# Low words behind the next scaling, the last pair's split inside the first FFN unit, and weight quarters loaded in two parts

## The chip, the cores and the metric

The kernel runs on one core of a Trainium2 chip. The metric is the device time of one execution in microseconds. Before the change the median of three runs is 844.63 us (843.42 to 845.4). Engines are called as in the profile: PE (TensorE matmul), PEld (its weight loads), DVE (VectorE), ACT (ScalarE), POOL (GpSimd), SP (SyncE, which here only issues DMAs).

## The reference

Three stages in a row, all in float32:

```
ret  = (q @ k.T / 8 * Dmat) @ v            # 4 batches x 8 heads, 576 tokens, head size 64; Dmat = gamma**(i-j) for i >= j
x    = ret as 2304 tokens x 512
h    = x @ w_in                            # FFN 1: 512 -> 2048
g    = (a0 + a1 h + a2 h^2 + a3 h^3) / (1 + |b0||h| + |b1| h^2 + 1e-6)
x2   = g @ w_out                           # 2048 -> 512
h2   = x2 @ w_in2;  y = (s * relu(h2)^2 + b) @ w_out2     # FFN 2
```

## The kernel before, in words

A full-precision product is built from three matmuls of a faster float type: each operand is cut into a high word and a low word, and the kernel multiplies high by low, low by high and high by high (`three`, L494 to L497). So every x, every g and every weight is written twice: an ACT copy rounds to the high word, and a subtraction (mostly on POOL) gives the low word.

**Retention** (`retention`, L214) works on 16 pairs p of two heads: batch p // 4, head pair p % 4. A pair's data come in two loads on the SP queue: `xT` (k and q, 576 KB, L256) and `vk` (v and k by chunks, 480 KB, L260), each in a ring of four buffers. The order is written out by hand with `pin` (keep in program order) on every engine. Iteration p of the loop at L407 holds, in this order:

- SP: the loads of pair p + 3, then a quarter of a raw weight tile (`next_quarter`, L143; 256 KB; 12 quarters in all, for weight tiles 0 to 2). The load of `xT` has to wait until `value_state(p - 1)` has read the buffer, the load of `vk` until `value_chunk(p - 1)` has.
- POOL: `scale(p + 2)` (L286), which multiplies v of pair p + 2 by decay factors and so waits for that pair's `vk` load.
- PE: `value_state(p)` (L350), `state(p + 1)` (L338, which reads the scaled v of pair p + 1), then `value_chunk(p)` (L358), and at the end `scores(p + 2)` (L315).
- ACT, DVE, POOL: one step (from p = 4 on) of `w_cut_in_halves` (L188), a generator of five steps per weight tile: bit arithmetic on DVE (L195, L199, L202), and twice per tile a high word on ACT (L165) with its low word on POOL (L166).
- DVE: the result x of pair p (L361); ACT: its high word `xh` (L365); POOL: its low word `xl` (L366). These two are `parts`, called straight after `value_chunk(p)`.

POOL therefore meets, in iteration p: `scale(p + 2)`, in some iterations a weight's low word, then `xl` of the same pair p. After the loop the steps of the weight cut that are still left are run off.

**FFN 1** (`ffn`, L443) goes through units u of 512 tokens and one 128-column tile of w_in. `emit_in` makes h on PE in one of four PSUM banks; `rational` (L540) is a chain over ACT (L546, L547, L549, L556, L558), POOL (L548) and DVE (L550, L551, L559 to L561), whose last step frees the bank; then g's words (L566, L568) and the products with w_out. The first three units are pinned as well. Unit 0 uses tokens 0 to 511, that is pairs 0 to 3 alone. On ACT and POOL it stands behind everything that retention issued, the last pair's `xh` and `xl` among it. **FFN 2** follows and is not touched.

Of the kernel before, what the change touches and what calls it, by code (L numbers as in the profile page):

```python
# [9 lines left out]
F32 = mybir.dt.float32  # L10
# [5 lines left out]
ALU = mybir.AluOpType  # L16
# [28 lines left out]
def retention_ffn_kernel(ctx, tc, a, b, s2, b2, w, qkv, maskv, gdec, out):  # L45
    nc = tc.nc
    B, H, S, D = SHAPE
    NT, DM = out.shape
    P = 128
# [7 lines left out]
    const = ctx.enter_context(tc.tile_pool(name="const", bufs=1))  # L57
# [11 lines left out]
    zeros = const.tile([P, P], F32, name="zeros")  # L69
    lnb = const.tile([P, 1], F32, name="lnb")  # L70
    expb = const.tile([P, 1], F32, name="expb")

    xh = xpool.tile([P, NC, NT], F32R, name="xh")
    xl = xpool.tile([P, NC, NT], F32R, name="xl")
# [4 lines left out]
    def f32(t):  # L79
        return t.bitcast(F32)  # L80
# [16 lines left out]
    def next_load(eng=nc.sync, pin=free):  # L97
        if w_ahead:
            loads[:] = loads[-1:] + [w_load(w_ahead.pop(0), eng, pin)]
# [27 lines left out]
    def w_place_raw(kf):  # L127
        w_raw[kf] = stg.tile([P, 2 * DM], I64, tag=raw_tag(kf), name=f"raw{kf}")
        return w_raw[kf]
# [8 lines left out]
    def next_quarter(pin):  # L138
        if quarters:
            kf, x = quarters.pop(0)  # L140
            t = w_raw[kf] if x else w_place_raw(kf)
            cols = slice(DM // 2 * x, DM // 2 * (x + 1))
            pin(nc.sync.dma_start(out=t[:, cols], in_=w[kf][:, cols]))  # L143

    def w_words(kf):
        words = w_raw[kf].bitcast(I32).rearrange("p (n two) -> p n two", two=2)
# [65 lines left out]
    NPAIR = len(pairs)  # L212

    def retention(actx):  # L214

        sbt = actx.enter_context(tc.tile_pool(name="sbt", bufs=2))
# [30 lines left out]
        pin = tc.keep_in_program_order  # L247
        pe = dve = pin
        rows = [slice(Q * j, Q * j + Q) for j in range(2)]
# [12 lines left out]
        def main_v(p):  # L262
            return vk[p][:, 0:NM].rearrange("p (c h d) -> p c h d", c=NMAIN, h=2)

        def tail_v(p):
            return vk[p][:, NM:MIX]
# [4 lines left out]
        def loads(p):  # L271
            if p < NPAIR:
                load_x(p)
                load_vk(p)
# [4 lines left out]
        def decay(hp):  # L279
            for k, (t0, t1) in enumerate(((P, 2 * P), (2 * P, 4 * P), (4 * P, S))):  # L280
                pin(nc.scalar.activation(odec[:, hp, t0:t1], odec[:, hp, 0:t1 - t0], AF.Copy, scale=powers[:, k, hp:hp + 1]))

        def scale(p, eng=nc.gpsimd):
            if p < NPAIR:
                hp = pairs[p][1]
                pin(eng.tensor_tensor(out=main_v(p), in0=main_v(p), op=ALU.mult,  # L286
                                      in1=vdec[:, :, 2 * hp:2 * hp + 2].unsqueeze(3).to_broadcast([P, NMAIN, 2, D])))

        def scale_tail(p):
            hp = pairs[p][1]  # L290
            pin(nc.scalar.activation(tail_v(p), tail_v(p), AF.Copy, scale=vdec_tail[:, hp:hp + 1]))
# [15 lines left out]
        def place(c):  # L307
            return 0 if c is None else Q + c * P
# [36 lines left out]
        def value_state(p):  # L345
            for c in range(1, NMAIN):

                cs = slice(c * P, S if c == NMAIN - 1 else (c + 1) * P)
                for r in rows:
                    pe(nc.tensor.matmul(pv[p][r, O0 + cs.start:O0 + cs.stop], lhsT=spre[p % 2][r, c - 1, :], rhs=xT[p][r, 1, cs],  # L350
                                        start=c in (1, NMAIN - 1), stop=True, skip_group_check=True))

        def value_chunk(p):
            bb, hp = pairs[p]
            v = main_v(p)
            for c, q0, q1 in [(c, c * P, S if c == NMAIN - 1 else (c + 1) * P) for c in range(NMAIN)] + [(None, NM, S)]:
                for j, r in enumerate(rows):
                    pe(nc.tensor.matmul(pv[p][r, O0 + q0:O0 + q1], lhsT=tail_v(p) if c is None else v[:, c, j, :],  # L358
                                        rhs=pm[p][:, j, place(c):place(c) + q1 - q0], start=False, stop=True, skip_group_check=True))
            x = sbt.tile([P, S], F32, tag="x", name=f"x{p}")  # L360
            dve(nc.vector.tensor_tensor(out=x, in0=pv[p][:, O0:O0 + S], in1=odec[:, hp], op=ALU.mult))  # L361
            xs = slice(bb * S, (bb + 1) * S)

            def parts():
                pin(nc.scalar.copy(xh[:, hp, xs], x))  # L365
                pin(nc.gpsimd.tensor_tensor(out=xl[:, hp, xs], in0=x, in1=f32(xh[:, hp, xs]), op=ALU.subtract))  # L366

            return parts

# [23 lines left out]
        steps = (s for kf in range(W_FIRST) for s in w_cut_in_halves(kf))  # L393
# [10 lines left out]
        tails()  # L404
        decay(0)
        scale(1)
        for p in range(NPAIR):  # L407
            if p:
                loads(p - 1 + IN_BUFS)
            for _ in range((1, 1, 2, 0)[p] if p < 4 else 1):  # L410
                next_quarter(pin)
            if p in (13, 14):
                next_load(nc.sync, pin)
            if p == 12:
                small_loads()
            scale(p + 2)
            value_state(p)
            if p == 0:
                scores(1)()

            if p < 2:
                parts = value_chunk(p)
            if p < NPAIR - 1:
                state(p + 1)
                scale_tail(p + 1)
            for _ in range((p > 3) + (p == 14)):
                next(steps, None)
            if p > 1:
                parts = value_chunk(p)
            parts()  # L430
            if p + 1 < NP:
                decay(p + 1)
            if p == 14:
                pin(nc.scalar.activation(babs, b_sb, AF.Abs))
                pin(nc.vector.tensor_scalar(aneg, a_sb, -1.0, None, op0=ALU.mult))
            if p + 2 < NPAIR:
                scores(p + 2)()
        for _ in steps:
            pass
        assert not quarters  # L440


    def ffn(fctx):  # L443
        accp = fctx.enter_context(tc.tile_pool(name="accp", bufs=1))
        gp = fctx.enter_context(tc.tile_pool(name="gp", bufs=1))

# [93 lines left out]
        def rational(u):  # L540

            pin = pe if u < 3 else free
            h = hps[u]
            ta, tq, tt = [tmp_tile(u, x) for x in ("ta", "tq", "tt")]
            with behind(*parts_at[1:2]):
                pin(nc.scalar.activation(ta, h, AF.Abs))  # L546
            pin(nc.scalar.activation(tq, ta, AF.Identity, bias=babs[:, 0:1], scale=babs[:, 1:2]))  # L547
            pin(nc.gpsimd.tensor_tensor(out=tq, in0=tq, in1=ta, op=ALU.mult))  # L548
            pin(nc.scalar.activation(tt, h, AF.Identity, bias=aneg[:, 2:3], scale=aneg[:, 3:4]))  # L549
            pin(nc.vector.tensor_tensor(out=tt, in0=tt, in1=h, op=ALU.mult))  # L550
            x = pin(nc.vector.scalar_tensor_tensor(out=tt, in0=tt, scalar=aneg[:, 1:2], in1=h, op0=ALU.add, op1=ALU.mult))  # L551
            if u == 2:
                third.append(x)
            if parts_of:
                parts_of.pop()(pe)
            pin(nc.scalar.activation(ta, tq, AF.Ln, bias=lnb, scale=QS))  # L556
            r = hps.pop(u)
            exp = pin(nc.scalar.activation(r, ta, AF.Exp, bias=expb, scale=-1.0))  # L558
            pin(nc.vector.scalar_tensor_tensor(out=tt, in0=tt, scalar=aneg[:, 0:1], in1=r, op0=ALU.add, op1=ALU.mult))  # L559
            pin(nc.vector.scalar_tensor_tensor(out=r, in0=tq, scalar=QC, in1=r, op0=ALU.add, op1=ALU.mult))  # L560
            end = pin(nc.vector.scalar_tensor_tensor(out=tt, in0=r, scalar=-2.0, in1=tt, op0=ALU.add, op1=ALU.mult))  # L561
            ends[:] = [end, exp, *ends[2:]]

            def parts(pin=free):
                gh, gl = g_tiles(u)
                parts_at.append(nc.scalar.copy(gh, tt))  # L566
                ends[1:] = [pin(parts_at[-1]),
                            pin(nc.gpsimd.tensor_tensor(out=gl, in0=tt, in1=f32(gh), op=ALU.subtract))]  # L568

            if u < 3:  # L570
                parts_of.append(parts)
            else:
                parts()
            if u == 3:
                with behind(*ends):
                    w_split_half(W_FIRST - 1, 1, free)
                del w_raw[W_FIRST - 1]
                next_load()
# [432 lines left out]
        for u in range(NU):  # L1011
# [14 lines left out]
            if final[0:1024].all() and len(sums) > (1 if u == NU - 1 else 2):  # L1026
                x = sums.pop(0)
# [25 lines left out]
    nc.vector.memset(lnb, QC * QS)  # L1053
    nc.vector.memset(expb, float(-24.0 * np.log(2.0)))
    with ExitStack() as actx:
        retention(actx)
    with ExitStack() as fctx:
        ffn(fctx)


_INS = ["moe_a", "moe_b", "moe2_s", "moe2_b"]
# [72 lines left out]
```

## Time and profile before

| | before |
|---|---|
| median of three runs | 844.63 us |
| the profiled execution: its time, its span | 845.24 us, 843.3 us |
| PE busy | 833.5 us (99%) |
| PEld, DVE, ACT, POOL busy | 703.6, 616.2, 600.1, 393.6 us |
| granted TensorE clock | 1.00 over the span |
| loaded and stored by DMA | 109.17 MB, mean 129 GB/s |

Times inside the profile count from the start of the span. A busy share says when an engine had an instruction in flight; matmuls overlap, so the pitch from one start to the next says more of PE than its busy time. "A <- B" in a list of waits reads "A stood idle until B was done"; "issue" is idle time that the profile can't lay to anything. SPq is the DMA queue of SyncE: a row of it is one issue, and "to landing" is the time from the issue until the data are there.

### The profile page before, as it was taken

Reading aid. Unit: us, or ns where it says so; the run is one execution under the profiler, and the core shown is the slowest. Engines: PE = TensorE matmul, PEld = TensorE weight load, DVE = VectorE, ACT = ScalarE, POOL = GpSimd, SP = SyncE. Lnnn points to the kernel's source line nnn. Section 1 sums busy time; section 2 is a strip of 40 time slices with the busy share of each in tenths; the row PEclk is TensorE's granted clock in tenths of the full one; section 3 lists DMA queues with packets and bytes.
Section 4 is the critical chain, followed back from the end, with each engine's and each line's share of the span. In section 5 each row is a group of like instructions: output and inputs, shape, how many; then the busy total and the mean of one; then the engine's idle time right before and its main releaser. Section 6 shows DMA issues by size and latency. Waiting matters only on the chain.

```text
span 843.3 us, 13082 instructions
## 1 busy us (share of the span) xinstructions
PE 833.5 (99%) x4966; PEld 703.6 (83%) x4966; DVE 616.2 (73%) x859; ACT 600.1 (71%) x991; POOL 393.6 (47%) x324
## 2 busy tenths in 40 slices
PE   8999999999999999999999999999999999999998
PEld 7887788888888888888888888888888888888887
DVE  4786987697798879789968867788777543444445
ACT  4446998687788778789979886686667766555553
POOL 3785675555567655548856423344235221111100
PEclk9999999999999999999999999999999999999999
DMA  9982120101102101101111377545699984444302
GB/s 343 346 318 88 50 101 1 64 37 50 51 1 101 49 2 51 50 1 51 51 51 33 68 249 250 191 168 167 224 310 365 232 241 150 149 150 150 126 0 100
DMA packets 38174, 109.17 MB, mean 129 GB/s; under 512 B 3936, under 2 KB 4704, under 8 KB 33504
## 3 DMA queue, kind: packets, MB, share of 16 engines
q1 hardware_dynamic: 27104, 79.44, 26.9%
q0 software_dynamic: 10864, 28.31, 11.8%
q8 instruction: 39, 0.64, 0.3%
q10 hardware_dynamic: 144, 0.59, 0.2%
q14 instruction: 23, 0.19, 0.1%
HBM read 75.30 MB, written 28.84 MB: 123 GB/s over the span
## 4 chain that ended last, share of the span: by engine, by line
PE 90%; DVE 4%; DMA 2%; POOL 1%; issue 1%; ACT 1%; SPq 0%; ACTq 0%; DVEq 0%; POOLq 0%
PE p L497 23%; PE o L497 23%; PE h L497 21%; PE hB L497 7%; PE hA L497 5%; PE hG L497 5%; PE ht L497 3%; PE hs L497 3%; DMA vk<-in_qkv_dram 2%; PE pv L358 1%; POOL vk L286 1%; DVE pm L328 1%; DVE tt L559 0%; PE sc L315 0%; PE pv L338 0%
## 5 line engine op out<-in xcount | busy, mean ns | idle before, releaser
L497 PE MATMUL h<-xh,w 128*128 128x512 f32 (+1 forms) x640 | 184.5, 368 | 0.0
L497 PE MATMUL o<-gh,w 128*128 128x512 f32 (+1 forms) x584 | 165.9, 369 | 0.0
L548 POOL TENSOR_TENSOR tq<-tq,ta 128x512 f32<-128x512 f32 x72 | 98.1, 1363 | 99.1 <-ACT tq L547 92.9
L815 DVE TENSOR_TENSOR acc<-acc,p 128x512 f32<-128x512 f32 (+1 forms) x127 | 86.3, 680 | 72.8 <-PE p L497 71.8
L497 PEld LDWEIGHTS h<-xh,w 128*128 128x128 f32 x640 | 116.2, 188 | 20.4
L497 PE MATMUL p<-w,gh 128*128 128x512 f32 (+1 forms) x338 | 124.3, 388 | 0.0
L497 PEld LDWEIGHTS o<-gh,w 128*128 128x128 f32 x584 | 106.1, 189 | 18.4
L497 PE MATMUL h<-xl,w 128*128 128x512 f32 (+1 forms) x320 | 118.2, 369 | 0.5 <-DVE tt L561 0.4
L497 PE MATMUL o<-gl,w 128*128 128x512 f32 (+1 forms) x292 | 107.8, 369 | 0.0
L568 POOL TENSOR_TENSOR gl<-tt,gh 128x512 fp32r<-128x512 f32 x66 | 92.8, 1407 | 30.4 <-ACT gh L566 25.9
L497 PE MATMUL p<-w,gx 128*128 128x512 f32 (+1 forms) x363 | 99.3, 387 | 0.0
L166 POOL TENSOR_TENSOR w<-raw,w 128x512 fp32r<-128x512 f32 x38 | 55.2, 1477 | 82.4 <-ACT w L165 29.0
L497 PEld LDWEIGHTS p<-w,gx 128*128 128x128 f32 x363 | 67.9, 188 | 13.9
L559 DVE SCALAR_TENSOR_TENSOR tt<-tt,aneg,h 128x512 f32<-128x512 f32 x72 | 53.5, 743 | 31.2 <-ACT h L558 30.9
L497 PEld LDWEIGHTS p<-w,gh 128*128 128x128 f32 x338 | 63.5, 188 | 13.1
L497 PEld LDWEIGHTS h<-xl,w 128*128 128x128 f32 x320 | 60.3, 188 | 11.8 <-DVE tt L561 1.1
L556 ACT ACTIVATE ta<-tq,lnb 128x512 f32<-128x512 f32 x72 | 52.3, 727 | 21.8 <-POOL tq L548 20.9
L497 PE MATMUL p<-w,gl 128*128 128x512 f32 (+1 forms) x169 | 65.5, 388 | 0.0
L779 ACT ACTIVATE ta<-hG 128x512 f32<-128x512 f32 x14 | 8.4, 598 | 76.9 <-PE hG L497 76.9
L497 PEld LDWEIGHTS o<-gl,w 128*128 128x128 f32 x292 | 55.1, 189 | 9.6 <-POOL gl L568 0.4
L550 DVE TENSOR_TENSOR tt<-tt,h 128x512 f32<-128x512 f32 x72 | 49.0, 681 | 18.3 <-ACT tt L549 18.0
L546 ACT ACTIVATE ta<-h 128x512 f32<-128x512 f32 x72 | 43.0, 597 | 24.3 <-PE h L497 23.9
(149 smaller groups left out, 1812.1 us busy)
## 6 DMA issues: line engine op xcount, KB each, us to landing
raw<-in_w_dram SPq DMA_DIRECT2D x29, 1024.0 KB, 5.3
ws<-w SPq DMA_DIRECT2D x32, 512.0 KB, 8.4
w<-ws POOLq DMA_DIRECT2D x32, 512.0 KB, 5.5
xT<-in_qkv_dram SPq DMA_DIRECT2D x15, 576.0 KB, 7.5
vk<-in_qkv_dram SPq DMA_DIRECT2D x16, 480.0 KB, 7.0
sf<-ss POOLq DMA_DIRECT2D x7, 1024.0 KB, 5.1
out_dram<-acc SPq DMA_DIRECT2D x17, 256.0 KB, 2.6
acc<-acc POOLq DMA_DIRECT2D x8, 512.0 KB, 4.6
```

The source lines that it names most:

```text
L166: pin(nc.gpsimd.tensor_tensor(out=dst[:, 1], in0=src, in1=f32(dst[:, 0]), op=ALU.subtract))
L286: pin(eng.tensor_tensor(out=main_v(p), in0=main_v(p), op=ALU.mult, in1=vdec[:, :, 2 * hp:2 * hp + 2].unsqueeze(3).to_broadcast([P, NMAIN, ...
L328: dve(nc.vector.tensor_tensor(out=t[:, :, 0:S], in0=sc[:, :, M0:M0 + S], op=ALU.mult, in1=mask.unsqueeze(1).to_broadcast([P, 2, S])))
L358: pe(nc.tensor.matmul(pv[p][r, O0 + q0:O0 + q1], lhsT=tail_v(p) if c is None else v[:, c, j, :], rhs=pm[p][:, j, place(c):place(c) + q1 - ...
L497: yield nc.tensor.matmul(ps, lhsT=lh, rhs=rh, start=start and x == 0, stop=stop and x == 2, skip_group_check=True)
L546: pin(nc.scalar.activation(ta, h, AF.Abs))
L548: pin(nc.gpsimd.tensor_tensor(out=tq, in0=tq, in1=ta, op=ALU.mult))
L550: pin(nc.vector.tensor_tensor(out=tt, in0=tt, in1=h, op=ALU.mult))
L556: pin(nc.scalar.activation(ta, tq, AF.Ln, bias=lnb, scale=QS))
L559: pin(nc.vector.scalar_tensor_tensor(out=tt, in0=tt, scalar=aneg[:, 0:1], in1=r, op0=ALU.add, op1=ALU.mult))
L568: pin(nc.gpsimd.tensor_tensor(out=gl, in0=tt, in1=f32(gh), op=ALU.subtract))]
L815: nc.vector.tensor_tensor(out=at, in0=at, in1=ps, op=ALU.add)
```

## The change

Three edits. `parts()` now only makes the high word and hands back the low word's subtraction, which is issued in the next iteration behind `scale(p + 2)`. The last pair has neither in the loop: its x goes to a tile of its own, and its high and low words are issued inside unit 0 of `rational`, behind ACT's L549; all steps of the weight cut that are left are run before `value_chunk` of the last pair instead of after its `parts`. And each quarter of a weight tile is loaded by two DMAs, rows 0 to 119 and rows 120 to 127, instead of one.

```diff
--- before.py
+++ after.py
@@ -69,6 +69,7 @@
     zeros = const.tile([P, P], F32, name="zeros")
     lnb = const.tile([P, 1], F32, name="lnb")
     expb = const.tile([P, 1], F32, name="expb")
+    x_last = const.tile([P, S], F32, name="x_last")
 
     xh = xpool.tile([P, NC, NT], F32R, name="xh")
     xl = xpool.tile([P, NC, NT], F32R, name="xl")
@@ -140,7 +141,9 @@
             kf, x = quarters.pop(0)
             t = w_raw[kf] if x else w_place_raw(kf)
             cols = slice(DM // 2 * x, DM // 2 * (x + 1))
-            pin(nc.sync.dma_start(out=t[:, cols], in_=w[kf][:, cols]))
+
+            for rows in (slice(0, 120), slice(120, P)):
+                pin(nc.sync.dma_start(out=t[rows, cols], in_=w[kf][rows, cols]))
 
     def w_words(kf):
         words = w_raw[kf].bitcast(I32).rearrange("p (n two) -> p n two", two=2)
@@ -357,13 +360,13 @@
                 for j, r in enumerate(rows):
                     pe(nc.tensor.matmul(pv[p][r, O0 + q0:O0 + q1], lhsT=tail_v(p) if c is None else v[:, c, j, :],
                                         rhs=pm[p][:, j, place(c):place(c) + q1 - q0], start=False, stop=True, skip_group_check=True))
-            x = sbt.tile([P, S], F32, tag="x", name=f"x{p}")
+            x = x_last if p == NPAIR - 1 else sbt.tile([P, S], F32, tag="x", name=f"x{p}")
             dve(nc.vector.tensor_tensor(out=x, in0=pv[p][:, O0:O0 + S], in1=odec[:, hp], op=ALU.mult))
             xs = slice(bb * S, (bb + 1) * S)
 
             def parts():
                 pin(nc.scalar.copy(xh[:, hp, xs], x))
-                pin(nc.gpsimd.tensor_tensor(out=xl[:, hp, xs], in0=x, in1=f32(xh[:, hp, xs]), op=ALU.subtract))
+                return lambda: pin(nc.gpsimd.tensor_tensor(out=xl[:, hp, xs], in0=x, in1=f32(xh[:, hp, xs]), op=ALU.subtract))
 
             return parts
 
@@ -404,6 +407,7 @@
         tails()
         decay(0)
         scale(1)
+        lows = []
         for p in range(NPAIR):
             if p:
                 loads(p - 1 + IN_BUFS)
@@ -414,6 +418,9 @@
             if p == 12:
                 small_loads()
             scale(p + 2)
+
+            for x in lows:
+                x()
             value_state(p)
             if p == 0:
                 scores(1)()
@@ -423,11 +430,12 @@
             if p < NPAIR - 1:
                 state(p + 1)
                 scale_tail(p + 1)
-            for _ in range((p > 3) + (p == 14)):
+            for _ in range((p > 3) + (p == 14) if p < NPAIR - 1 else 15):
                 next(steps, None)
             if p > 1:
                 parts = value_chunk(p)
-            parts()
+            if p < NPAIR - 1:
+                lows = [parts()]
             if p + 1 < NP:
                 decay(p + 1)
             if p == 14:
@@ -435,12 +443,11 @@
                 pin(nc.vector.tensor_scalar(aneg, a_sb, -1.0, None, op0=ALU.mult))
             if p + 2 < NPAIR:
                 scores(p + 2)()
-        for _ in steps:
-            pass
         assert not quarters
-
-
-    def ffn(fctx):
+        return parts
+
+
+    def ffn(fctx, last_parts):
         accp = fctx.enter_context(tc.tile_pool(name="accp", bufs=1))
         gp = fctx.enter_context(tc.tile_pool(name="gp", bufs=1))
 
@@ -547,6 +554,8 @@
             pin(nc.scalar.activation(tq, ta, AF.Identity, bias=babs[:, 0:1], scale=babs[:, 1:2]))
             pin(nc.gpsimd.tensor_tensor(out=tq, in0=tq, in1=ta, op=ALU.mult))
             pin(nc.scalar.activation(tt, h, AF.Identity, bias=aneg[:, 2:3], scale=aneg[:, 3:4]))
+            if u == 0:
+                last_parts()()
             pin(nc.vector.tensor_tensor(out=tt, in0=tt, in1=h, op=ALU.mult))
             x = pin(nc.vector.scalar_tensor_tensor(out=tt, in0=tt, scalar=aneg[:, 1:2], in1=h, op0=ALU.add, op1=ALU.mult))
             if u == 2:
@@ -1053,9 +1062,9 @@
     nc.vector.memset(lnb, QC * QS)
     nc.vector.memset(expb, float(-24.0 * np.log(2.0)))
     with ExitStack() as actx:
-        retention(actx)
+        last_parts = retention(actx)
     with ExitStack() as fctx:
-        ffn(fctx)
+        ffn(fctx, last_parts)
 
 
 _INS = ["moe_a", "moe_b", "moe2_s", "moe2_b"]
```

## Rows read from the trace of the kernel before

**Rows 1.** Engines by stage: busy time and instructions, granted clock, DMA share, GB/s

```profile
10.00:20.00 10.00, 9.42 (x222) 8.40 (x217) 6.01 (x8) 5.86 (x19) 5.84 (x5) 1.00 1.03 404
24.00:66.00 42.00, 39.72 (x894) 34.92 (x890) 34.03 (x43) 19.88 (x50) 34.00 (x26) 1.00 0.90 323
72.00:96.00 24.00, 23.70 (x107) 18.62 (x104) 19.87 (x31) 21.03 (x33) 12.88 (x11) 1.00 0.00 1
```

**Rows 2.** Timeline of PE, `value_chunk` of pairs 3, 4 and 14: start, duration

```profile
24.08 1.27 PE L358 MATMUL pv<-pm,vk 128*64 128x128 f32 x20
27.59 1.27 PE L358 MATMUL pv<-pm,vk 128*64 128x128 f32 x20
...
65.78 1.27 PE L358 MATMUL pv<-pm,vk 128*64 128x128 f32 x20
```

**Rows 3.** Waits of PE from 20 to 67: us in total, times, longest

```profile
PE pv L350 <- issue: 1.5, 2, 1.1
PE pv L338 <- POOL vk L286: 1.2, 3, 0.4
PE sc L315 <- issue: 0.6, 1, 0.6
```

**Rows 4.** Timeline of POOL around iteration 6: start, duration

```profile
36.20 1.50 POOL L286 TENSOR_TENSOR vk<-vk,mv 128x512 f32<-128x512 f32 x1
37.66 1.30 POOL L166 TENSOR_TENSOR w<-raw,w 128x512 fp32r<-128x512 f32 x1
38.92 1.40 POOL L366 TENSOR_TENSOR xl<-x,xh 128x576 fp32r<-128x576 f32 x1
40.29 1.49 POOL L286 TENSOR_TENSOR vk<-vk,mv 128x512 f32<-128x512 f32 x1
```

**Rows 5.** The load of vk of pair 8: duration of the issue, its start, time to landing

```profile
L260 SPq DMA_DIRECT2D vk<-in_qkv_dram x1: 327/327/327, 29.0 to 29.0; - x1
...
DMA to landing us min/median/max: 6.9/6.9/6.9
```

**Rows 6.** DMA from 24 to 66: queues (packets, MB, share of 16 engines), issues (KB, landing)

```profile
q1 hardware_dynamic: 4638, 13.44, 88.6%
q8 instruction: 7, 0.11, 1.5%
...
xT<-in_qkv_dram SPq DMA_DIRECT2D x9, 576.0 KB, 7.3
```

**Rows 7.** Waits of the SP queue from 6 to 24

```profile
SPq L143 <- DMA odec<-in_gdec_dram: 0.5, 1, 0.5
```

**Rows 8.** Timeline of the SP queue from 1.5 to 7.2: start, duration

```profile
1.67 0.42 SPq L277 DMA_DIRECT2D odec<-in_gdec_dram  x1
...
6.91 0.33 SPq L143 DMA_DIRECT2D raw<-in_w_dram  x1
```

**Rows 9.** Timeline of ACT from 69 to 74, with idle before and releaser

```profile
69.91 0.65 ACT L165 CAST w<-raw 128x512 fp32r<-128x512 f32 x1
73.30 0.68 ACT L365 CAST xh<-x 128x576 fp32r<-128x576 f32 x1 [2.74 <-DVE x L361]
73.88 0.59 ACT L546 ACTIVATE ta<-h 128x512 f32<-128x512 f32 x1
```

**Rows 10.** Timeline of DVE from 72 to 75

```profile
72.50 0.76 DVE L361 TENSOR_TENSOR x<-pv,odec 128x576 f32<-128x576 f32 x1 [2.65 <-PE pv L358]
73.18 0.68 DVE L199 SCALAR_TENSOR_TENSOR wm<-wm,raw 128x512 uint32<-128x512 uint32 x1
```

**Rows 11.** Timeline of PE in FFN 1, matmuls of three units

```profile
79.97 0.61 PE L497 MATMUL h<-xh,w 128*128 128x512 f32 x2
80.78 0.50 PE L497 MATMUL h<-xl,w 128*128 128x512 f32 x1 [0.20 <-DVE tt L561]
...
97.93 0.39 PE L497 MATMUL h<-xl,w 128*128 128x512 f32 x1
...
108.81 0.39 PE L497 MATMUL h<-xl,w 128*128 128x512 f32 x1
```

## Prediction

> **What bounds the kernel now.** Two lines first. The page gives PE 833.5 of 843.3 us busy, so what an edit can win is what PE loses, and it has to be found stage by stage. The table of stages [rows 1] shows where: from 24 to 66 PE is busy 39.72 of 42 us, from 72 to 96 23.70 of 24; both are stretches in which this change edits something. Busy time hides more, since matmuls overlap, so I read pitches next. "Same" below means within 0.2% of the median (1.7 us), about what a measurement of this kernel can tell from no change.
>
> In retention the same 68 or so matmuls come round once a pair. From `value_chunk` of pair 3 to that of pair 4 is 27.59 - 24.08 = 3.51 us [rows 2], a round in which PE waited for nothing. From pair 4 to pair 14 is 65.78 - 27.59 = 38.19 us for ten rounds, 3.82 each: 3.1 us more than ten rounds of 3.51. The list of PE's waits [rows 3] names 1.2 us of it as `state` waiting for POOL's scaling, three times; of the waits on "issue" the longest, 1.1 us, lies ahead of these rounds, which leaves 1.5 - 1.1 + 0.6 = 1.0 us inside them. The other 0.9 us is not named; part of it is the refill of PE's pipeline after each wait.
>
> POOL's rows say why the scaling is late [rows 4]: in iteration 6 it does scaling, a weight's low word and xl, 1.50 + 1.30 + 1.40 = 4.2 us by their durations, and the next scaling starts at 40.29, 4.09 after the last. That is more than a round of 3.51. In iterations without a weight's low word the load is 1.50 + 1.40 = 2.9, but POOL can't use the 0.6 us to get ahead, because xl(p) stands behind xh(p) of the same iteration. The loads are a second limit close behind: pair 8's vk is issued at 29.0 and lands after 6.9, at 35.9 [rows 5], and its scaling starts at 36.20 [rows 4].
>
> In FFN 1 the timeline of PE [rows 11] has 48 matmuls from 97.93 to 108.81, 0.2267 each. From 79.97 to 97.93 there are 74 (2, then six groups of 12), which at that pitch are 16.77 us; they took 17.96. So 1.2 us is lost, the first of it at 80.78, where unit 4 waits for the PSUM bank that unit 0's last DVE step frees. Unit 0's chain began late: ACT's L546 is at 73.88, straight behind xh of the last pair at 73.30, for which ACT had stood idle 2.74 us [rows 9] because DVE's x waited for PE until 72.50 [rows 10].
>
> **Term 1, the low word behind the next scaling.** Nothing is added or removed; POOL's order changes. xl(p - 1) then has its xh long before, so POOL no longer idles for ACT, and the two kinds of iteration average (4.2 + 2.9) / 2 = 3.55; iterations with a weight's low word are five of the last ten, and the 1.0 us of "issue" widens some rounds, so POOL can hold PE's pace if it may get about half a microsecond ahead. Whether it may depends on the loads (term 2). If it may, the 1.2 us of waits go and, with them, most of the unnamed 0.9: I take 1.8. Ends: 0, if the loads land no earlier, and 3.1, if everything above 3.51 goes.
>
> **Term 2, the quarter in two parts.** It adds 12 issues on SP, 0.33 us each by the row at 6.91 [rows 8], 4.0 us in all; SP mostly stands waiting for PE to release buffers, which covers them; without that cover each would delay the next pair's loads by 0.33. For the loads themselves the rows show no single DMA engine. [...] One thing could make a single engine slow: instruction fetches [rows 6], 7 packets in 42 us that took 1.5% of 16 x 42, 10 us of engine time. In a round of 3.82 that is 0.9 us. A quarter's share of one engine is 16 KB at q1's rate (0.886 x 672 us for 13.44 MB, 44 us a MB), 0.7 us. [...] At PE's pitch of 3.51 a pair's 1.34 MB ask 383 GB/s; 404 were moved from 10 to 20 [rows 1]. [...]
>
> **Term 3, the last pair inside unit 0.** ACT no longer waits for x of pair 15 before L546. It is free after the weight's high word at 69.91 + 0.65 = 70.56 [rows 9], so L546 can start up to 73.88 - 70.56 = 3.3 us earlier. POOL's product for unit 0 no longer stands behind xl. The moved xh stands behind L549 (about 2 us later, 72.6), waits for x until 73.3 and is done near 73.9, while POOL works on unit 0's product: no cost. xl, 1.40 [rows 4], follows that product, and unit 1's is not ready yet. DVE's two steps of the weight cut (0.68 at 73.18 [rows 10], so some 1.4 together) move ahead of x into its 2.65 us of idle time: no cost, and DVE is free for unit 0 as soon as x is done. PE's 1.2 us between 80 and 98 are chains that are late by 0.2 to 0.5 us each; 3 us of lead covers them. I take 1.2; ends 0 and 1.7 (a like wait later in FFN 1 might shrink too).
>
> **Sum.** 1.8 + 1.2 = 3.0 us: from the profiled execution's 845.24 (span 843.3, 1.9 around it) to 842.2. That execution is 0.6 above the median of 844.63; carried to the median, 841.6 us.
>
> **Rivals.**
> *The loads land no earlier* (25%). [...] Then scaling 8 can't start before 35.9 [rows 5], and with 4.2 us of POOL work behind it the next starts at 40.1 against 40.29: term 1 is worth 0.2 in each of a few rounds, and only term 3 is left: 844.63 - 1.2 = 843.4. For it: landing and scaling are 0.3 apart. [...]
>
> *Slower: the SP queue runs out of open loads* (10%). SP waits for landings of loads that have nothing to do with the next one: the first quarter at 6.91 waited for odec [rows 7], and the first odec load was issued at 1.67 [rows 8], eight issues before (seven rows lie between; a second odec load is among them, which is the other reading). If no more than eight loads may be open, they now cover 8 / 3 rounds, 10.2 us at 3.82; with four loads a pair they cover two rounds, and a pair's xT waits until the xT of two pairs earlier has landed. The round is then at least half the landing time: at the median of 7.3 [rows 6] 3.65, harmless; it decides from 2 x 3.82 = 7.6 on. Should landings stretch to 8.5, rounds are 4.25, ten of them cost 4.3 more, less term 3: 844.63 + 3.1 = 847.7. Against it: fewer open loads also queue less.
>
> *The first chain doesn't move* (10%): unit 0's buffers may lie where retention's were, so that its first writes wait for the last pair's readers, and ACT starts near 72.5 to 73.3 still. Term 1 alone: 842.8.
>
> *More goes than I count* (15%): the waits on "issue" in rounds 20 to 67, 1.5 + 0.6 = 2.1 [rows 3], shrink with quicker fetches, and 0.5 of later waits go: 841.6 - 2.6 = 839.0.
>
> **How the numbers follow.** The forecast has 40%. Faster by over 0.2% (under 842.9): nearly all of the forecast, all of the fourth rival, half of the third: 0.36 + 0.15 + 0.05 and a little of the first, 0.58. Same: most of the first, half of the third, the rest of the forecast, 0.31. Slower (over 846.3): the second and chance reordering of FFN 1's unpinned work, 0.11. The range holds the forecast with its ends, the first and third rival and the nearer half of the fourth: 839.4 to 845.5.
>
> **What would show it.** Right: POOL's xl behind the scaling, no wait of `state` for POOL, rounds near 3.6 between pairs 4 and 14; L546 of unit 0 near 70.6 and no wait at the matmul of unit 4; landing times under 6.5. Wrong: landings as before with rounds still at 3.8 (first rival); SP waiting for `xT` or `vk` landings in every round (second); L546 still past 72.5 (third); or a new stall of PE beyond 110 us, which nothing here covers.

## The result and the profile after

The changed kernel takes 851.84 us, median of 4 runs (850.4 to 852.75), beside 844.02 for the kernel before (842.68 to 845.4): ratio 1.0088, 95% interval 1.0071 to 1.0105. The medians are 7.8 us apart, and the interval lies clear of no change; forecast were 841.6 us and a range of 839.4 to 845.5. The profiled execution has a span of 850.5 us (843.3 before).

First the stages of the changed kernel, as in [rows 1]: busy time and instructions of PE, PEld, DVE, ACT and POOL, granted clock, DMA share, GB/s.

```profile
10.00:20.00 10.00, 9.41 (x214) 8.31 (x206) 6.01 (x8) 5.55 (x17) 4.10 (x4) 1.00 1.05 344
24.00:66.00 42.00, 35.49 (x772) 30.45 (x771) 27.65 (x38) 17.67 (x43) 26.13 (x22) 1.00 1.03 302
72.00:96.00 24.00, 22.96 (x149) 18.62 (x147) 19.56 (x27) 17.57 (x29) 18.48 (x13) 1.00 0.14 49
```

From 24 to 66 PE lost 4.2 us of busy time against [rows 1], and DVE and POOL fell too: nobody became busier except the DMA engines, whose share rose from 0.90 to 1.03 while the bytes per second fell from 323 to 302. Busier and slower at once: each byte took longer.

The starts of `value_chunk` (L361 now) for pairs 3, 4 and 14 and the first matmul of FFN 1, in PE's timeline after:

```profile
24.01 1.27 PE L361 MATMUL pv<-pm,vk 128*64 128x128 f32 x20
28.55 1.27 PE L361 MATMUL pv<-pm,vk 128*64 128x128 f32 x20
...
73.93 1.27 PE L361 MATMUL pv<-pm,vk 128*64 128x128 f32 x20
75.12 0.50 PE L504 MATMUL h<-xl,w 128*128 128x512 f32 x1
```

Pair 3 starts as before (24.08 in [rows 2]); pair 14 starts at 73.93 and not at 65.78. So 8.2 us are lost between these two, and the ten rounds from pair 4 on take 45.38 us, 4.54 each (3.82 before). Behind retention 1.0 us of them comes back, which makes the span's 7.2 (850.5 - 843.3).

What POOL waits for after, from 20 to 67 (us in total, times, longest):

```profile
POOL vk L289 <- DMA vk<-in_qkv_dram: 15.9, 9, 2.7
```

The largest wait of the SP queue before, in the same stretch:

```profile
SPq L260 <- PE pv L358: 13.8, 10, 1.9
```

And after:

```profile
SPq L259 <- DMA xT<-in_qkv_dram: 10.7, 8, 2.0
SPq L263 <- DMA vk<-in_qkv_dram: 6.2, 8, 1.3
SPq L146 <- DMA raw<-in_w_dram: 4.7, 7, 0.7
```

The DMA view after, from 24 to 66 (columns as in [rows 6]):

```profile
q1 hardware_dynamic: 4074, 12.57, 101.7%
...
xT<-in_qkv_dram SPq DMA_DIRECT2D x9, 576.0 KB, 9.0
vk<-in_qkv_dram SPq DMA_DIRECT2D x9, 480.0 KB, 9.0
raw<-in_w_dram SPq DMA_DIRECT2D x8, 240.0 KB, 9.1
```

POOL's scaling now waits 15.9 us for landings of v, nine times (0.9 us, once, before). SP, which before held a pair's loads back until PE had released a buffer, now waits for landings: xT for an earlier xT, vk for an earlier vk, a quarter for an earlier quarter. A pair's xT lands after 9.0 us where [rows 6] had 7.3. The chain that ended last says the same in one column (start, duration):

```profile
17.19 9.59 DMA vk<-in_qkv_dram
26.87 8.27 DMA vk<-in_qkv_dram
35.23 9.03 DMA vk<-in_qkv_dram
...
62.38 9.79 DMA vk<-in_qkv_dram
```

Six loads of vk, one behind the other, cover 17 to 72 us; each spans about two rounds of 4.54. In SP's timeline each of the later ones is issued 0.1 us behind the landing of the load eight issues before it (26.87 behind a landing at 26.79, 35.23 behind 35.14), so no more than eight loads are open; no run shows whether the chip or the program sets that. It looks exactly like the second rival (a round of half the landing time). The experiments ask whether this rule of eight is the cause or the consequence.

In FFN 1, ACT's first step of unit 0 (L553, L546 before) in its timeline after:

```profile
80.67 0.60 ACT L553 ACTIVATE ta<-h 128x512 f32<-128x512 f32 x1 [0.95 <-PE pv L361]
```

And PE's matmuls of the first units in its timeline after:

```profile
81.05 0.40 PE L504 MATMUL h<-xl,w 128*128 128x512 f32 x1
...
95.38 0.39 PE L504 MATMUL h<-xl,w 128*128 128x512 f32 x1
```

L553 starts 6.74 us behind the last but one `value_chunk` (80.67 - 73.93); before it was 73.88 - 65.78 = 8.1 [rows 2, 9]. That is 1.4 us earlier and not the forecast 3.3, and the row says why: ACT waited for PE's last `value_chunk`, which ended at 80.54. The 63 matmuls from 81.05 to 95.38 are 0.2275 apart, where the same stretch had lost 1.2 us before [rows 11]: the gain came all the same.

### The profile page after: what moved, and what is told of

Read it like the earlier page. It is cut to its first block, busy times and chain, and to the rows that moved or that the text cites. A ratio compares the mean times of both kernels' runs of the same rounds, so it can differ in the third digit from the quotient of the medians.

```text
span 850.5 us, 13101 instructions
## 1 busy us (share of the span) xinstructions
PE 833.9 (98%) x4966; PEld 703.9 (83%) x4966; DVE 616.9 (73%) x859; ACT 601.0 (71%) x991; POOL 392.4 (46%) x324
## 4 chain that ended last, share of the span: by engine, by line
PE 91%; DMA 6%; DVE 1%; ACT 0%; POOL 0%; issue 0%; SPq 0%; DVEq 0%; POOLq 0%
PE p L504 23%; PE o L504 23%; PE h L504 23%; PE hB L504 7%; DMA vk<-in_qkv_dram 6%; PE hA L504 4%; PE hG L504 4%; PE ht L504 3%; PE hs L504 3%; PE sc L383 1%; PE pv L361 0%; PE sc L318 0%; DVE pm L331 0%; PE pv L353 0%; DVE acc L608 0%; DVE tt L568 0%
## 5 line engine op out<-in xcount | busy, mean ns | idle before, releaser
L504 PEld LDWEIGHTS h<-xh,w 128*128 128x128 f32 x640 | 116.2, 188 | 20.3
L169 POOL TENSOR_TENSOR w<-raw,w 128x512 fp32r<-128x512 f32 x38 | 57.1, 1528 | 81.1 <-ACT w L168 41.1
L565 ACT ACTIVATE ta<-tq,lnb 128x512 f32<-128x512 f32 x72 | 52.2, 725 | 20.6 <-POOL tq L555 19.7
L553 ACT ACTIVATE ta<-h 128x512 f32<-128x512 f32 x72 | 42.9, 595 | 25.5 <-PE h L504 24.1
```

What stands on the lines that cost most here:

```text
L169: pin(nc.gpsimd.tensor_tensor(out=dst[:, 1], in0=src, in1=f32(dst[:, 0]), op=ALU.subtract))
L504: yield nc.tensor.matmul(ps, lhsT=lh, rhs=rh, start=start and x == 0, stop=stop and x == 2, skip_group_check=True)
```

## The experiments

All ratios are to the kernel before, run beside them on the same chip.

### Which edit costs the time

Whole quarters again, the other two edits kept:

```diff
-            for rows in (slice(0, 120), slice(120, P)):
-                pin(nc.sync.dma_start(out=t[rows, cols], in_=w[kf][rows, cols]))
+            pin(nc.sync.dma_start(out=t[:, cols], in_=w[kf][:, cols]))
```

> The changed kernel with every quarter loaded whole again (128 rows, one DMA); the two other edits stay. Theory A (open loads): the loss comes from four loads a pair against a limit of eight open ones, so it goes: 842 to 844 us, SP waits for PE again and not for landings. Theory B (slow packets): the loss comes from the 120-row loads, whose packets and those beside them take longer, so it goes as well: the same time, and the packets' rate is back at about 44 us of engine time a MB or less. Theory C (the loads are innocent, POOL's new order costs it): still above 850 us.

And the other way round, the split quarters alone in the kernel before (the same lines, plus and minus exchanged):

> The kernel before with nothing but the quarters loaded as 120 and 8 rows. A and B: all of the loss and none of what the last pair's move gives, 851 to 854 us; SP waits for landings of xT and vk in every round. C: 843 to 845 us.

Measured: 845.05 us, 0.9999 (0.9978 to 1.0019), with whole quarters; 853.45 us, 1.0105 (1.0071 to 1.0139), with the split alone. The split is the whole loss, and theory C falls. The stage from 24 to 66 with whole quarters:

```profile
24.00:66.00 42.00, 37.95 (x846) 33.25 (x845) 34.85 (x42) 19.41 (x48) 34.35 (x27) 1.00 0.88 321
```

The same stage with the split alone:

```profile
24.00:66.00 42.00, 34.86 (x726) 30.11 (x725) 27.12 (x35) 16.98 (x41) 26.10 (x22) 0.96 1.03 299
```

And the DMA view of that stage with the split alone:

```profile
q1 hardware_dynamic: 4047, 12.44, 101.8%
...
xT<-in_qkv_dram SPq DMA_DIRECT2D x10, 576.0 KB, 8.7
```

With whole quarters the DMA share is 0.88 at 321 GB/s, as before the change; with the split it is 1.03 at 299, as after. But without the split the other two edits win nothing either, and the profile with whole quarters is no copy of the one before: its ten rounds from pair 4 to pair 14 take 67.10 - 26.26 = 40.8 us (38.2 before), with 4.2 us of PE's waits named "issue" in them (1.0 before). That is taken up further down.

### Too many loads, or loads of too few rows

Two loads per quarter again, cut by columns (224 and 32), all 128 rows in both, so that SP issues and counts as many as in the change:

```diff
-            for rows in (slice(0, 120), slice(120, P)):
-                pin(nc.sync.dma_start(out=t[rows, cols], in_=w[kf][rows, cols]))
+            for c in (slice(cols.start, cols.stop - 32), slice(cols.stop - 32, cols.stop)):
+                pin(nc.sync.dma_start(out=t[:, c], in_=w[kf][:, c]))
```

> The changed kernel with each quarter still loaded by two DMAs, but cut by columns (224 and 32 of 256), so that both have all 128 rows. A (four loads a pair are one too many): as slow as the changed kernel, 849 to 853 us, with SP waiting for landings in every round. B (the shape of 120 rows is what hurts): 842 to 845 us, the rate in the rounds back above 320 GB/s, landings near 7 us.

And the reverse: 120 rows per quarter, the other 8 rows once for the whole tile, 15 loads and not 24:

```diff
-            for rows in (slice(0, 120), slice(120, P)):
-                pin(nc.sync.dma_start(out=t[rows, cols], in_=w[kf][rows, cols]))
+            pin(nc.sync.dma_start(out=t[0:120, cols], in_=w[kf][0:120, cols]))
+            if x == 0:
+                pin(nc.sync.dma_start(out=t[120:P], in_=w[kf][120:P]))
```

> The changed kernel with rows 0 to 119 loaded quarter by quarter as in it, but rows 120 to 127 of a tile by one DMA for all its columns: 15 loads of weights in retention instead of 24 (12 before). A: most of the loss gone, 843 to 846 us. B: most of the loss stays, 848 to 852 us, the rate near 300 GB/s in the rounds and landings of xT and vk at 8 us or more, though SP has hardly more loads open than before.

Measured: by columns 845.54 us, 1.0001 (0.9978 to 1.0023); with the eight rows once 854.2 us, 1.0116 (1.0093 to 1.014). The load of xT in the DMA view by columns, from 24 to 66:

```profile
xT<-in_qkv_dram SPq DMA_DIRECT2D x8, 576.0 KB, 6.0
```

SP's largest wait by columns, from 20 to 67:

```profile
SPq L263 <- PE pv L361: 13.3, 9, 2.0
```

The load of xT with the eight rows once:

```profile
xT<-in_qkv_dram SPq DMA_DIRECT2D x9, 576.0 KB, 10.2
```

SP's largest wait with the eight rows once:

```profile
SPq L264 <- PE pv L362: 15.9, 10, 2.6
```

With the change's number of loads but full rows, xT lands in 6.0 us and SP waits for PE. With fewer loads but 120 rows, xT takes 10.2 us, SP mostly waits for PE too, and the time is lost all the same (more than the 848 to 852 us that theory B gave). So the count of open loads is not the cause. The waits of SP for landings in the change are what slow loads make of the rule of eight, and taking most of them away doesn't help.

Is it 120 beside 8 rows, or do other loads short of 128 do the same? Halves of 64 rows:

```diff
-            for rows in (slice(0, 120), slice(120, P)):
+            for rows in (slice(0, 64), slice(64, P)):
```

> The changed kernel with each quarter loaded as rows 0 to 63 and rows 64 to 127. Theory B1 (a load of fewer than 128 rows deals its rows out to the DMA engines otherwise than a load of 128 rows, so that engines get in each other's way at the same rows of SBUF): as slow as the changed kernel or slower, 849 to 856 us, rate near 300 GB/s in the rounds. [...]

Measured: 853.96 us, 1.0113 (1.0079 to 1.0148); q1's loads took 102.8% of the engines' time for 11.96 MB in the 42 us. So it is not 120 and 8 alone: halves cost as much. B1 has the time right; what it says of DMA engines and rows of SBUF, no run shows.

The loads by themselves: a kernel with nothing but quarter loads on SP, as many as the queue takes, in five stages of 32 quarters (128 rows; 120; 120 and 128 in turn; 64 and 64; 112), DVE touching each tile when its four quarters have landed.

> Loads alone, no computation (the output is left at zero, everything of the reference is left out): five stages of 32 quarter loads each of 128 rows; of 120 rows; of 128 and 120 rows in turn; of 64 and 64 rows; of 112 rows. B1: the stages with fewer than 128 rows move clearly less per us than the first (350 GB/s or more there, 180 to 300 in the others), the mixed one too. [...] If 120 rows are as fast as 128 both alone and mixed, the slowing needs something else of the kernel, and B falls in this form.

The GB/s line of its DMA view (40 slices of 4.4 us):

```profile
GB/s 13 255 331 394 391 387 251 260 248 251 251 249 251 234 261 255 258 258 253 255 248 163 210 172 235 203 210 207 204 207 194 285 269 274 272 271 286 405 404 231
```

DVE's touches in its timeline, one per tile, two neighbours from each stage:

```profile
21.68 0.15 DVE L62 COPY gate<-raw 128x1 int32<-128x1 int32 x1 [2.39 <-DMA raw<-in_w_dram]
24.39 0.15 DVE L62 COPY gate<-raw 128x1 int32<-128x1 int32 x1 [2.55 <-DMA raw<-in_w_dram]
...
39.18 0.15 DVE L62 COPY gate<-raw 128x1 int32<-128x1 int32 x1 [3.77 <-DMA raw<-in_w_dram]
43.10 0.15 DVE L62 COPY gate<-raw 128x1 int32<-128x1 int32 x1 [3.77 <-DMA raw<-in_w_dram]
...
75.38 0.15 DVE L62 COPY gate<-raw 128x1 int32<-128x1 int32 x1 [3.84 <-DMA raw<-in_w_dram]
79.35 0.15 DVE L62 COPY gate<-raw 128x1 int32<-128x1 int32 x1 [3.81 <-DMA raw<-in_w_dram]
...
121.93 0.15 DVE L62 COPY gate<-raw 128x1 int32<-128x1 int32 x1 [4.87 <-DMA raw<-in_w_dram]
127.00 0.15 DVE L62 COPY gate<-raw 128x1 int32<-128x1 int32 x1 [4.91 <-DMA raw<-in_w_dram]
...
143.89 0.15 DVE L62 COPY gate<-raw 128x1 int32<-128x1 int32 x1 [3.24 <-DMA raw<-in_w_dram]
147.27 0.15 DVE L62 COPY gate<-raw 128x1 int32<-128x1 int32 x1 [3.22 <-DMA raw<-in_w_dram]
```

Per tile (four quarters): 128 rows 2.71 us for 1.049 MB, 387 GB/s; 120 rows 3.92 us for 0.983 MB, 251; 120 and 128 in turn 3.97 us for 1.016 MB, 256; two halves 5.07 us for 1.049 MB, 207; 112 rows 3.38 us for 0.918 MB, 272. The third stage matters most here: half of its loads are whole, and it is hardly faster than 120 rows alone. Had its whole loads kept 387 GB/s, a tile would have taken 3.3 us. At 3.97 us a tile, short loads slowed the full ones beside them.

In the change a pair asks for 1.344 MB, a fifth of it in quarters cut by rows. At the 387 GB/s of whole loads that is 3.5 us, at the 256 of the mixed stage 5.2; the rounds of 4.54 lie between, and two rates give no closer estimate. That the 302 GB/s of 24 to 66 give 4.45 us is no second proof, since that rate was measured in those very rounds. With POOL's 15.9 us of waits for landings, it says that retention has become bound by its loads.

No row here has the DMA engines singly: what slows a load of 120 rows, and why it is slower than 112, stays open.

### What the other two edits are worth

The low words behind the next scaling, alone in the kernel before:

```diff
-                pin(nc.gpsimd.tensor_tensor(out=xl[:, hp, xs], in0=x, in1=f32(xh[:, hp, xs]), op=ALU.subtract))
+                return lambda: pin(nc.gpsimd.tensor_tensor(out=xl[:, hp, xs], in0=x, in1=f32(xh[:, hp, xs]), op=ALU.subtract))
...
             scale(p + 2)
+            for x in lows:
+                x()
...
-            parts()
+            lows = [parts()]
...
+        for x in lows:
+            x()
```

> The kernel before with only POOL's order changed: the low word of x behind the next scaling; quarters whole, the last pair as before. Theory D (POOL's waits were replaced by waits on 'issue', which grow when rounds get shorter): 844 to 846 us against 844 to 845 before, no wait of state for POOL, more than 2.1 us of waits on 'issue'. Theory E (my term 1): 842.5 to 843.5 us.

The last pair inside unit 0, alone (the low words straight behind their high words, as before):

```diff
...
-            for _ in range((p > 3) + (p == 14)):
+            for _ in range((p > 3) + (p == 14) if p < NPAIR - 1 else 15):
...
-            parts()
+            if p < NPAIR - 1:
+                parts()()
...
-        for _ in steps:
-            pass
...
+            if u == 0:
+                last_parts()()
...
```

> The kernel before with only the last pair's words moved into unit 0 and the rest of the weight cut ahead of its chunk; quarters whole, POOL's order in the loop as before. Term 3 as forecast: 1.2 us less than before (1.0 to 1.5), PE's pitch between units 0 and 6 of FFN 1 at 0.227 us a matmul throughout. Rival: nothing, because what is won there is lost in later units.

Measured: low words alone 846.93 us, 1.0021 (1.0000 to 1.0041); last pair alone 844.48 us, 0.9989 (0.9969 to 1.0008). The last pair's edit takes PE's losses in FFN 1 away in the profile, and its forecast of 1.2 us (0.9986) lies inside the interval, but so does no change. The low words gave nothing: theory E's 842.5 to 843.5 us (a ratio of 0.999 at most) lies outside the interval. PE's waits of that run from 6 to 76:

```profile
PE pv L350 <- issue: 3.4, 2, 2.3
PE pv L338 <- issue: 2.8, 4, 1.0
```

`state` (L338) no longer waits for POOL: that much of the theory holds. It waits 2.8 us in all, four times, for something the profile calls "issue"; before it was 1.5 us for POOL, four times, in the same stretch. One such place in the timeline of that run, all engines (start, duration):

```profile
35.20 1.05 POOL L286 TENSOR_TENSOR vk<-vk,mv 128x512 f32<-128x512 f32 x1 [2.13 <-PE pv L338]
...
36.20 1.40 POOL L366 TENSOR_TENSOR xl<-x,xh 128x576 fp32r<-128x576 f32 x1
36.24 1.91 DVE L202 SCALAR_TENSOR_TENSOR raw<-raw,wm 128x512 uint32<-128x512 uint32 x1
...
38.08 0.74 DVE L361 TENSOR_TENSOR x<-pv,odec 128x576 f32<-128x576 f32 x1
...
38.92 0.33 PE L338 MATMUL pv<-vk 128*64 128x128 f32 x2 [0.96 <-issue]
```

DVE's x ends at 38.82 and `state` starts 0.10 later; x is the last reader of the PSUM tile that `state` writes next. The three other waits end 0.10 or 0.11 us behind an x as well. And x is late because the step of the weight cut ahead of it took 1.91 us: it began together with POOL's xl and ended 0.55 behind it. Such a step takes 0.78 in five of eight rounds of the kernel before; the eight between 30 and 66 us add up to 7.9 us there and to 11.0 in this run. The test takes xl away:

```diff
-                return lambda: pin(nc.gpsimd.tensor_tensor(out=xl[:, hp, xs], in0=x, in1=f32(xh[:, hp, xs]), op=ALU.subtract))
+                return None
...
+        for i in range(NC):
+            (nc.vector if i % 2 else nc.gpsimd).memset(f32(xl[:, i]), 0.0)
```

> The run with the low words alone, with the low word of x (POOL's L366, 1.40 us a round) left out: xl is filled with zeros at the start, so the output lacks the products with the low word of x. In that run the matmuls of state (L338) began 0.10 us after the end of DVE's x (L361) in the four rounds with a wait named issue (x ended at 34.27, 38.82, 46.64, 54.49; state began at 34.38, 38.92, 46.74, 54.59), and x stood behind a step of the weight cut (L199, L202) that took 0.95 to 1.91 us there and mostly 0.78 in the kernel before. Theory H: that step and POOL's xl read two SBUF operands each and hold each other up, so what term 1 took from POOL came back on DVE. Then without xl the cut steps take 0.78, except where the weight's low word (L166) lies beside them; the four waits of state, 2.8 us in all, go to under 0.6; and from the value_chunk of pair 4 to that of pair 14 it is at most 36.5 us, against 38.2 before. Theory G: TensorE's supply of instructions sets these waits, whatever DVE and POOL do. Then some 2 us of waits ahead of state stay and ten rounds take 37.5 or more. The waits inside lines (L350 after its third matmul near 21 us, after its eighth near 65) are left by either. The time of the whole kernel decides nothing, since FFN 1 has other work on POOL than before.

Measured: 844.93 us, 0.9985 (0.9957 to 1.0013). PE's largest waits from 6 to 76:

```profile
PE pv L350 <- issue: 2.0, 2, 1.2
PE sc L315 <- issue: 1.4, 2, 1.0
```

Two cut steps in DVE's timeline of that run:

```profile
35.21 0.69 DVE L202 SCALAR_TENSOR_TENSOR raw<-raw,wm 128x512 uint32<-128x512 uint32 x1
...
54.98 1.41 DVE L202 SCALAR_TENSOR_TENSOR raw<-raw,wm 128x512 uint32<-128x512 uint32 x1
```

The waits of `state` named "issue" are gone, and six of the eight cut steps between 30 and 66 take 0.68 to 0.69 us (the two others, 1.41 and 1.01, lie beside a scaling). So theory H is right on what stopped `state`. It is wrong on the sum: the ten rounds took 65.82 - 27.29 = 38.5 us, not at most 36.5. Seven of the ten are 3.51 to 3.67, but the waits inside lines are left, and grew: L315 now stops for 0.96 and 0.43 us (0.62 before), L350 for 0.79 (0.37).

Such waits inside a line lie behind few of its matmuls, the same ones in every version: in L350 behind the third of twelve near 21 us and behind the eighth near 64, in L315 behind the 18th or the 31st of 36, in some versions in `value_chunk` behind the fifth or the 18th of 20, in the changed kernel once in `state` behind the fourth of 12. One thing was tried on them: the two 1 MB weight loads, the first of which is open when the last of them falls, were moved behind the loop in the order of the program, once in the run with whole quarters and once in the run with the last pair alone.

```diff
-            if p in (13, 14):
-                next_load(nc.sync, pin)
...
+        for _ in range(2):
+            next_load(nc.sync, pin)
```

> The change with whole quarters, and the two 1 MB weight loads that the rounds of pairs 13 and 14 issue moved behind the last round. Of the waits on issue that took the place of the waits for POOL in the run with whole quarters, the longest, 1.7 us ahead of the matmuls of L351 at about 64 us, falls while those two loads (1024 KB each, 6.3 us to landing) are under way. Theory F: the loads hold back what the wait is for. Then the wait ahead of L351 near 64 us is under 0.6 us, the matmuls of L508 begin about 1.2 us earlier than 68.3 us, and the ratio is about 0.9985 (843.6 us beside 844.9). Theory G: TensorE's own pace of instructions sets the wait, whatever is loaded. Then 1.2 to 2.4 us are left there and the ratio is 0.999 to 1.001. By either, the weight tiles of these two loads are first needed far behind 100 us, so nothing in the second part waits for them.

> The run with the last pair alone (whole quarters, low words where they were before), with the same two 1 MB loads behind the last round. The run without the move had 0.9989 and waits on issue of 1.8, 0.9 and 0.4 us in the retention. Theory F: the wait near 64 to 68 us shrinks by about 1 us and the ratio is about 0.9975 (842.4 us beside 844.5): it is then faster than the kernel before and the change. Theory G: the ratio stays at 0.998 to 1.000.

Measured: 845.49 us, 1.0002 (0.9983 to 1.0022), and 845.2 us, 0.9996 (0.9972 to 1.002). But the move hardly moved the loads in time. The two issues in SP's timeline, with whole quarters (from the first to the end of the second):

```profile
57.14 8.66 SPq L134 DMA_DIRECT2D raw<-in_w_dram  x2
```

And in the same run with the move:

```profile
56.98 7.82 SPq L134 DMA_DIRECT2D raw<-in_w_dram  x2
```

So neither time decides between F and G. The wait near 63 us of the first of the two runs, in its list:

```profile
PE pv L351 <- issue: 2.3, 1, 2.3
```

What all DMA queues together moved from 63 to 64 us of that run:

```profile
DMA packets 14, 0.04 MB, mean 41 GB/s; under 512 B 10, under 2 KB 10, under 8 KB 10
```

L351 stands still there from 63.1 to 65.4 us. It is 8 GB/s from 64 to 65, and with whole quarters and no move 0 GB/s from 64.5 to 66, inside a wait of 1.7 us. Loads that move next to nothing don't hold anything back by their traffic, so theory F falls on these rows and not on the times. That the waits keep to one place of the program speaks for PE's supply of instructions. So does a packet of the instruction queue (q8, 0.02 MB) that begins 2.2 to 2.5 us before PE goes on, in three of them: between 63.0 and 63.2 us here (PE at 65.42), between 65.6 and 65.9 with the low words alone (68.06), between 20.3 and 20.6 in the kernel before (22.84). No run here shows that PE waits for it, and it stays open. No version that was tried is faster than the kernel before by more than its interval.

## Why the prediction was wrong

**Term 2, the quarter in two parts, is the step that failed.** It took the split for 12 more issues that SP has time for and for some relief of one DMA engine, which no run shows, since no row has the engines singly; its cost was set at nothing, and no end of the range stood for loads that are themselves slower. What a load costs by its number of rows was in no row of the trace before, and the text bounded only issues and bytes. Measured: 251 GB/s for 120 rows against 387, and 256 when every other load is whole. Nor does a run show the earlier landings that term 1's 1.8 us stood on: xT landed after 9.0 us in the change, 7.3 before. Ten rounds went from 3.82 to 4.54 us each, 7.2 of the 8.2 us. Not all of that need be the split's, since the ten rounds with whole quarters took 4.08 each in the profile, by PE's waits on issue; in the time of the whole kernel the split costs 0.9 to 1.05%, 7.5 to 8.9 us (1.0088 against 0.9999, and 1.0105 alone). The issues themselves cost nothing, as said: with two loads per quarter by columns the time is 1.0001.

**The second rival** had the side and, by its own relation, even the form: a landing of 9.0 us, rounds of half that, SP waiting for xT and vk in every round. Its mechanism falls all the same, since the same number of loads does no harm with full rows and fewer loads do as much with 120. It also had only 10%: against it stood that fewer open loads queue less, and the forecast wanted landings under 6.5 us.

**The first rival** had no loss: "lands no earlier" left 843.4 us, where the two parts by rows are slower than the whole; halves came to 1.0113. The parts don't only land no earlier: the 120 rows of a quarter took 9.1 us to landing, a whole quarter 7.1 before (both medians from 24 to 66).

**Term 1** (1.8 us) was wrong by itself. The waits of `state` for POOL do go; but xl now runs beside DVE's weight cut, whose step grows from 0.78 to as much as 1.91 us, and DVE's x is late in POOL's place. That pair was in the trace before: the scaling that takes 1.50 from 36.20 in [rows 4] stands beside a cut step of 36.01 to 36.79, and takes 1.05 in the run with the low words alone. The prediction took 1.50 for the work, when by these two some 0.45 of it was lost beside DVE's step. The other way round, the step that began at 36.24 beside an xl of 36.20 to 37.60 ended at 38.15, 1.91 us, where without xl it takes 0.69. If such rows run one behind the other, as these two nearly did (1.95 us for 1.40 + 0.69), an estimate of a round is 1.05 + 1.40, half of 1.30 for the weight's low word, and 0.69, 3.8 us, against rounds of 3.82 before: by that, POOL's order could not have brought more than a little.

**Term 3** has its gain, but not by its path. 1.2 us of PE's losses between 80 and 98 are gone, and no new stall stands beyond. But unit 0 did not start 3.3 us earlier: in the change, and with the last pair alone, ACT's first step waits for PE's last `value_chunk` and starts 6.74 us behind the last but one. Counted in the trace before, that is 65.78 + 6.74 = 72.5 us, the very sign of **the third rival** (the first chain doesn't move). So the rival had the start right; its price, no gain from term 3, was not, since 1.4 us earlier was enough. Whether buffers are the reason, as it says, no run shows. Nor were the steps of the weight cut free: the two ahead of the last x took 1.90 and 1.69 us in the change, beside POOL, where 1.4 together was reckoned, and x began at 82.48, 1.9 us behind PE's last `value_chunk`. In the total the term is too small to be told from nothing (0.9989, 0.9969 to 1.0008).

## What to carry to other kernels

Before a load is cut by rows, measure one with fewer rows: here 120 rows, 112 rows and twice 64 rows ran at 207 to 272 GB/s against 387, and 120 rows pulled the whole loads beside it down with it; cut by columns, the same two loads cost nothing. When a queue begins to wait for landings, vary the number of loads and their form separately before blaming the queue. Read in the trace whether a load that was moved in the program has moved in time. And before work is moved from one moment to another on POOL, look at which DVE instruction it will then meet: a long POOL or DVE row may hold time lost beside the other, as the 1.50 us scaling and the 1.91 us step did here, and moving it moves the loss.

## What the runs showed that was not expected

- Full loads slow down beside short ones: 256 GB/s with every other load whole, 251 with none. Among short ones 112 rows (272) beat 120 (251), and both beat two halves (207).
- One xl of 1.40 us more than doubles a DVE step of 0.69 us that starts 0.04 us later.
- TensorE's clock fell during retention or just behind it in six of the twelve profiled executions of the whole kernel (a mean of 0.998 over each of the six), not in those of the kernel before and the change. With the split alone, PE was busy 3.82 of 6 us from 54 to 60, and in the next 6 us the granted clock was 0.72 on average:

```profile
54.00:60.00 6.00, 3.82 (x86) 3.30 (x84) 2.92 (x5) 1.84 (x5) 3.81 (x4) 1.00 1.04 288
60.00:66.00 6.00, 6.00 (x96) 5.16 (x94) 3.85 (x5) 2.12 (x5) 3.39 (x4) 0.72 1.03 274
```

By that mean, 0.28 x 6 us, an estimate is up to 1.7 us less work there. Whether the split alone is slower than the whole change (853.45 against 851.84) is not shown, since the two intervals overlap (1.0071 to 1.0139, 1.0071 to 1.0105). Executions of one kernel differ with the clock by more than the two other edits are worth: with the last pair alone and the big loads behind the loop, five of twelve have a mean granted clock of 1.000 and take 841.55 to 843.43 us, six have 0.998 or less and take 846.82 to 848.72; of the kernel before beside them, fifteen of 23 with 1.000 take 842.78 to 846.83 us, six with 0.998 or less 846.89 to 848.61.
